# Reordering the first pair of an attention kernel: maxima ahead of differences, ScalarE's order by hand

## The chip, the cores and the metric

The kernel runs on one core of a Trainium2 chip. Its time is that of one execution on the device, in microseconds (us), from runs of the whole program. The core has five engines, each with its own queue of instructions: TensorE (PE in the profile; PEld is its loading of weights), VectorE (DVE), ScalarE (ACT), GpSimd (POOL) and SyncE (SP). SP only issues DMAs; ScalarE and GpSimd can issue them too (ACTq, and POOL's queue).

## The reference

Attention with a mask in blocks of 64, and behind it a gated MLP with a last projection:

```python
scores = scale * np.matmul(q, k.transpose(0, 1, 3, 2))     # q, k, v: 8 batches, 8 heads, 576, 64
scores = np.where(block_i >= block_j, scores, -1e9)        # blocks of 64 positions
scores = scores - np.max(scores, axis=-1, keepdims=True)
attn = np.exp(scores)
attn = attn / (np.sum(attn, axis=-1, keepdims=True) + 1e-09)
x = np.matmul(attn, v)                  # then laid out as 4608 tokens x 512
a = x @ w1                              # 512 x 1024
b = x @ w2                              # 512 x 1024
h = a * b @ w3                          # 1024 x 1024
return h @ w_out                        # 1024 x 512
```

The weights come as 64-bit floats; q, k and v as 32-bit floats.

## The kernel before, in words

**Work and stages.** The heads are taken in 32 pairs, four to a batch. A pair's two heads (j = 0, 1) lie in the two halves of the partitions. The first four pairs (EARLY) run beside the loading and unpacking of the weights; then the weights' working space is closed, and 28 pairs run with the MLP of the batch before filling TensorE. The MLP of the last batch ends the program. w3 and w_out are multiplied with each other once, in the early stage (gen_prod), so that the MLP has three weights: w1, w2 and the product w.

**A pair.** shift_mask(n) casts k (kb) and q (qd) to 16 bits on ScalarE, multiplies them in six groups (tiles mx) and takes each block's maximum on VectorE (line 196); a transpose (mt), a negation on ScalarE (ms, line 202) and shift put the negated maxima into rows of the tile qk. In pair 0, shift is a product on VectorE with rows of constants (line 213); in the others it is a small DMA on ScalarE's queue (line 218). prep_qk(n, j) casts q and k into a high part (line 166, VectorE), copies that to the other half (lines 229 and 230 in pair 0, DMAs at 232 and 233 in others) and forms the low part by a difference (line 235). s_tiles makes the scores in five tiles (line 265, two products for each part) with exponentials on ScalarE (line 273, pe). pv_early multiplies them with the values (line 304; ve holds the values and a half of ones that gives the sums). take_early, norm and finish_x divide and split the result.

**Weights.** load_w takes one load of 512 KB: a DMA on SP into one of five buffers wraw, two passes on ScalarE (lines 150 and 151), one on GpSimd (152) and one on VectorE (153). There are 40: eight of w_out (tile wo), sixteen of w3 (two for each of eight blocks m, in two buffers), and eight each of w1 and w2, whose values are split into a high and a low part on GpSimd and VectorE (161, 162). gen_w hands them out in order: before, w_out first, then w3's first two blocks, then w1, w2 and further blocks of w3 as their buffers come free. gen_prod multiplies block by block; one step is two products (four matmul records in the profile), 32 steps in all.

**Order.** TensorE's order is that of the program's text (manual_schedule). For the other engines a planner orders the instructions by priority and by its own model of time; steps of the early pairs have a raised priority, weights haven't. The order around a pair is written out by hand in a string for each head: B is a step of prep_qk(n, 1), M of shift_mask(n + 1), A of prep_qk(n + 1, 0), S a tile of scores, V a value product, C a step of gen_w, W a step of gen_prod, Q the values' casts of the next pair and the load of the pair after it, N and T the end of a head and of the pair. Ahead of the first pair stands:

```python
    fill(shift_mask(0), 100)
    fill(prep_qk(0, 0), 100)
    for j in range(2):
        prep_v(0, j)
    weights = gen_w(wp)
    fill(weights, 2)
    load(1)
```

fill(g, k) takes k steps of g. A step of gen_w before is two loads.

## Time and profile before

| what | value |
|---|---|
| time, median of 3 runs (lowest to highest) | 971.45 us (969.41 to 972.49) |
| the profiled execution: time, span | 970.15 us, 968.3 us |
| mean granted TensorE clock | 0.996 |
| busy, share of the span: TensorE, VectorE, ScalarE, GpSimd | 97%, 72%, 57%, 64% |
| TensorE busy in the first 20 us | 4.9 us |
| TensorE busy from 20 to 120 us | 88.8 us |
| TensorE busy from 140 to 900 us | all of it |
| first matmul of the MLP (line 426) | at 137.17 us |
| DMA engines busy, first 60 us | 80% to 99% in each 10 us |

The profile comes from one execution, 1.3 us under the median. Its span runs from the first to the last instruction; the time has 1.85 us around it. All times in rows are us from the start of the span. A row of the timeline gives start, duration, engine, line, operation, the tiles out<-in, their shape, how many instructions are merged, and in brackets how long the engine was idle before, with what ended that. A busy TensorE is not TensorE at its peak, since matmuls overlap.

### The profile page before, as it was taken

Reading aid. Unit: us, or ns where it says so; the run is one execution under the profiler, and the core shown is the slowest. Engines: PE = TensorE matmul, PEld = TensorE weight load, DVE = VectorE, ACT = ScalarE, POOL = GpSimd, SP = SyncE. Lnnn points to the kernel's source line nnn. Section 1 sums busy time; section 2 is a strip of 40 time slices with the busy share of each in tenths; the row PEclk is TensorE's granted clock in tenths of the full one; section 3 lists DMA queues with packets and bytes.
Section 4 is the critical chain, followed back from the end, with each engine's and each line's share of the span. In section 5 each row is a group of like instructions: output and inputs, shape, how many; then the busy total and the mean of one; then the engine's idle time right before and its main releaser. Section 6 shows DMA issues by size and latency. Waiting matters only on the chain.

```text
span 968.3 us, 18335 instructions
## 1 busy us (share of the span) xinstructions
PE 938.8 (97%) x6624; PEld 878.7 (91%) x6624; DVE 692.3 (72%) x1230; ACT 556.6 (57%) x1451; POOL 617.5 (64%) x605
## 2 busy tenths in 40 slices
PE   3898899999999999999999999999999999999998
PEld 1454469999999999999999999999999999999998
DVE  6787767788777777787787777777887777774100
ACT  7768736556565556565656555565555656553221
POOL 6766737677766767677776767676777667672211
PEclk9899999999999999999999999999999999999999
DMA  8976512212212221321222222222122122100000
GB/s 303 305 230 204 158 51 64 86 32 72 76 58 82 65 88 52 88 65 47 66 76 64 71 81 64 78 61 88 33 69 75 58 82 64 50 13 26 7 20 26
DMA packets 31303, 79.81 MB, mean 82 GB/s; under 512 B 5356, under 2 KB 13676, under 8 KB 31212
## 3 DMA queue, kind: packets, MB, share of 16 engines
q1 hardware_dynamic: 29788, 76.26, 25.7%
q10 hardware_dynamic: 1424, 2.38, 1.0%
q8 instruction: 52, 0.85, 0.4%
q14 instruction: 39, 0.32, 0.1%
HBM read 50.76 MB, written 9.44 MB: 62 GB/s over the span
## 4 chain that ended last, share of the span: by engine, by line
PE 89%; ACT 3%; DVE 3%; POOL 2%; issue 1%; DMA 1%; ACTq 0%; SPq 0%; DVEq 0%; POOLq 0%
PE ab L426 42%; PE o L442 21%; PE s L265 9%; PE x L320 9%; PE mx L192 4%; PE w L407 2%; POOL wbits L152 1%; ACT wbits L151 1%; ACT wy L150 1%; PE x L304 1%; DVE m L196 1%; ACT pe L273 1%; DMA qk<-ms 1%; DVE w L153 0%; PE tot L337 0%
## 5 line engine op out<-in xcount | busy, mean ns | idle before, releaser
L286 POOL TENSOR_TENSOR rsum<-rsum,p 128x448 f32<-128x448 f32 x224 | 185.8, 829 | 86.8 <-ACT p L280 78.3
L283 DVE TENSOR_TENSOR pl<-p,ph 128x448 fp32r<-128x448 f32 x168 | 149.4, 903 | 59.9 <-ACT ph L281 59.0
L435 POOL TENSOR_TENSOR gl<-g,gh 128x288 fp32r<-128x288 f32 x128 | 114.4, 894 | 121.9 <-ACT gh L434 121.9
L265 PE MATMUL s<-qk 128*128 128x288 f32 (+4 forms) x768 | 155.2, 311 | 6.1 <-ACT pe L273 3.6
L235 POOL TENSOR_TENSOR qk<-raw,qk 64x1152 fp32r<-64x1152 f32 x58 | 155.0, 2673 | 8.6 <-issue 5.6
L426 PE MATMUL ab<-xh,w2h 128*128 128x288 f32 x512 | 153.8, 300 | 0.0
L442 PE MATMUL o<-gh,wh 128*128 128x288 f32 x512 | 153.6, 300 | 0.0
L426 PE MATMUL ab<-xh,w1h 128*128 128x288 f32 x512 | 151.1, 295 | 0.0
L426 PE MATMUL ab<-xl,w2h 128*128 128x288 f32 x512 | 151.0, 295 | 0.0
L426 PE MATMUL ab<-xl,w1h 128*128 128x288 f32 x512 | 151.0, 295 | 0.0
L426 PE MATMUL ab<-xh,w1l 128*128 128x288 f32 x512 | 150.9, 295 | 0.0
L426 PE MATMUL ab<-xh,w2l 128*128 128x288 f32 x512 | 150.9, 295 | 0.0
L442 PE MATMUL o<-gh,wl 128*128 128x288 f32 x512 | 150.9, 295 | 0.0
L442 PE MATMUL o<-gl,wh 128*128 128x288 f32 x512 | 150.8, 295 | 0.0
L434 ACT CAST gh<-g 128x288 fp32r<-128x288 f32 x128 | 55.4, 433 | 143.1 <-DVE g L433 143.0
L265 PEld LDWEIGHTS s<-qk 128*128 128x128 f32 (+1 forms) x768 | 116.0, 182 | 17.9 <-ACT pe L273 9.4
L281 ACT ACTIVATE ph<-s 128x288 fp32r<-128x288 f32 x336 | 131.5, 393 | 0.0
L196 DVE TENSOR_REDUCE m<-mx 128x1 f32<-128x64 f32 (+3 forms) x320 | 128.4, 447 | 2.2 <-PE mx L192 0.2
L280 ACT ACTIVATE p<-s 128x448 f32<-128x448 f32 x224 | 85.4, 381 | 51.2 <-PE s L265 50.4
L283 DVE TENSOR_TENSOR pl<-rsum,ph 128x288 fp32r<-128x288 f32 x112 | 75.6, 676 | 49.6 <-ACT ph L281 45.6
L320 PE MATMUL x<-ph,vs 128*128 128x128 f32 x336 | 110.4, 329 | 0.0
L433 DVE TENSOR_TENSOR g<-ab,a 128x288 f32<-128x288 f32 x128 | 56.6, 442 | 69.8 <-PE ab L426 69.0
(76 smaller groups left out, 2180.4 us busy)
## 6 DMA issues: line engine op xcount, KB each, us to landing
raw<-in_qkv SPq DMA_DIRECT2D x31, 896.0 KB
qk<-qk SPq DMA_DIRECT2D x108, 144.0 KB
out_t<-o SPq DMA_DIRECT2D x64, 144.0 KB
wraw<-in_w3t SPq DMA_DIRECT2D x16, 512.0 KB
wraw<-in_w SPq DMA_DIRECT2D x16, 512.0 KB
wraw<-in_wout SPq DMA_DIRECT2D x8, 512.0 KB
qk<-qk ACTq DMA_DIRECT2D x16, 144.0 KB
qk<-ms SPq DMA_DIRECT2D x54, 2.2 KB
```

The source lines that it names most:

```text
L196: nc.vector.reduce_max(m[:, col : col + 1], sc, axis=AX.X)
L235: (nc.gpsimd if "late" in tl or n * j else nc.vector).tensor_tensor(out=qk[j][o, 2:4], in0=rqk[o], in1=qk[j][o, 0:2], op=ALU.subtract)
L265: nc.tensor.matmul(t[ks, at : at + q1 - q0], qk[j][:, k, kr], qk[j][:, q, q0:q1], start=(s == 0), stop=(s == 1))
L280: nc.scalar.activation(p32, t[ks, at : at + w], AF.Exp, scale=SCALE)
L281: nc.scalar.activation(ph[ks, o : o + w], t[ks, at : at + w], AF.Exp, scale=SCALE)
L283: nc.vector.tensor_tensor(out=low, in0=p32, in1=ph[ks, o : o + w], op=ALU.subtract)
L286: nc.gpsimd.tensor_tensor(out=r, in0=r, in1=p32, op=ALU.add)
L320: nc.tensor.matmul(xps[:, to : to + w], v[:, c, :], pr[:, a : a + w], start=(u < 2 and s == 0), stop=(u in (0, len(PV) - 1) and s == len(p ...
L426: nc.tensor.matmul(t[:, 0:HALF], l[:, c, fs], r, start=(c == 0 and s == 0), stop=(c == NC - 1 and s == 2))
L433: nc.vector.tensor_tensor(out=g32, in0=acc[1][:, 0:HALF], in1=a32, op=ALU.mult)
L435: nc.gpsimd.tensor_tensor(out=gl[:, f, :], in0=g32, in1=gh[:, f, :], op=ALU.subtract)
L442: nc.tensor.matmul(t[:, 0:HALF], l[:, f, es], r[:, f, :], start=(f == 0 and s == 0), stop=(f == NF - 1 and s == 2))
```

## The change

It touches the start and the first two pairs.

- The constants' rows (144 KB for each of two tables) went by SP into a scratch tile and by four copies on GpSimd into the tiles qk; now two DMAs on GpSimd's queue write them straight into qk, one for each head and both tables (288 KB each).
- The differences of pair 0 move from VectorE to GpSimd (both heads), and the copies of head 0 from ScalarE to VectorE.
- The values of pairs 0 and 1 are loaded apart from q and k, later (load_v).
- From the casts of pair 0 to the end of its first head ScalarE too is kept in the order of the text. The first six groups of maxima stand in it, then head 0's prep_qk, then two weight loads (the first block of w3), then the rest of the shift.
- In pair 0's first head three score tiles stand ahead of the masks of pair 1, and these are cut finer (a step before each cast of q).
- gen_w steps by one load (c; C is two), hands out w3's first two blocks first, then w_out, and further blocks of w3 as soon as their buffer allows. Ahead of pair 0 there are two loads instead of four; pair 0 takes eight in both, so ten instead of twelve have been handed out by its end.
- gen_prod takes blocks 0 and 1 together, row by row of w_out, so that its first step needs both blocks of w3 and one row of w_out. Pair 0 has four W instead of two, pair 1 eight instead of nine.

```diff
@@ -49,10 +49,10 @@
 )
 
 EARLY_PLAN = (
-    ("B B M S S B M S M S C M S M V V C V V V Q N",
-     "M S S A C S M S A C S V V A M V V V Q N T W W"),
-    ("B B C M S S W B M S S M W C S M W V V M V V V Q N",
-     "M S S A C W S M S A W C S W V V A M V V V C Q N T W W W"),
+    ("B B S S S M V S M V S M B c V M c V M V C M Q N",
+     "S S A C S W M S A S W A M V V W C M V W V M V Q N T"),
+    ("B B C M S S W B M S S M W C S M W V V M W V V V Q N",
+     "M S S A C S M S A C S W V V A M V V W V C Q N T W W"),
     ("B B M S S W C B M S S M W C S M W V V M V V V Q N",
      "M S S A W C S M S A W C S W V V A M V V V Q N T W W W C"),
     ("B B C M S S W B M S S M W C S M W V V M V V V Q N",
@@ -101,17 +101,17 @@
     def load(n):
         t = raws.tile([P, RAW], F32, tag="raw", name=f"raw{n}")
         src = qkv[n // NPAIR, n % NPAIR]
-        for cs in (slice(S, 2 * S), slice(0, S), slice(2 * S, RAW)) if n == 0 else (slice(0, RAW),):
+        raw_of[n] = t
+        for cs in (slice(S, 2 * S), slice(0, S)) if n == 0 else (slice(0, 2 * S),) if n == 1 else (slice(0, RAW),):
             nc.sync.dma_start(out=t[:, cs], in_=src[:, cs])
-        raw_of[n] = t
+
+    def load_v(n):
+        nc.sync.dma_start(out=raw_of[n][:, 2 * S :], in_=qkv[n // NPAIR, n % NPAIR][:, 2 * S :])
 
     load(0)
-    for t, tag in enumerate(("tr", "x32")):
-        cst = work.tile([P, S], F32, tag=tag, name=f"cst{t}")
-        nc.sync.dma_start(out=cst[0:D], in_=consts[:, t * S : (t + 1) * S])
-        for j in range(2):
-            nc.gpsimd.tensor_copy(qk[j][oth[j], 3 * t, :], cst[0:D])
     nc.sync.dma_start(out=both, in_=ident_in)
+    for j in range(2):
+        nc.gpsimd.dma_start(out=qk[j][oth[j], 0:4:3, :], in_=consts.rearrange("p (t s) -> p t s", t=2))
     nc.gpsimd.memset(qd, 0.0)
 
     tl = {}
@@ -177,6 +177,8 @@
         kb = work.tile([P, S], BF16, tag="kb", name=f"kb{n}")
         cast(n, kb, rqk[:, 1, :], CAST[1])
         for j in range(2):
+            if n == 1:
+                yield
             cast(n, qd[own[j], :, own[j]], rqk[own[j], 0, :].rearrange("p (i r) -> p i r", r=BLK), CAST[2])
         yield
         m = work.tile([P, 32], F32, tag="m", name=f"m{n}")
@@ -225,14 +227,14 @@
         cast(n, qk[j][o, 0:2], rqk[o], CAST[0])
         yield
         if n == 0:
-            copy = nc.gpsimd.tensor_copy if j else nc.scalar.copy
+            copy = (nc.gpsimd if j else nc.vector).tensor_copy
             copy(qk[j][x, 1, :], rqk[o, 1, :])
             copy(qk[j][x, 2, :], rqk[o, 0, :])
         else:
             queue(n).dma_start(out=qk[j][x, 1, :].bitcast(F32), in_=qk[j][o, 1, :].bitcast(F32))
             queue(n).dma_start(out=qk[j][x, 2, :].bitcast(F32), in_=qk[j][o, 0, :].bitcast(F32))
         yield
-        (nc.gpsimd if "late" in tl or n * j else nc.vector).tensor_tensor(out=qk[j][o, 2:4], in0=rqk[o], in1=qk[j][o, 0:2], op=ALU.subtract)
+        (nc.gpsimd if "late" in tl or n == 0 or j else nc.vector).tensor_tensor(out=qk[j][o, 2:4], in0=rqk[o], in1=qk[j][o, 0:2], op=ALU.subtract)
         yield
 
     def prep_v(n, j):
@@ -375,42 +377,61 @@
         def rows(u):
             for k in range(2 * u, 2 * u + 2):
                 load_w(tl["wo"][:, k, :], wout[k])
+                yield
 
         def w3(m):
             assert done[0] >= m - 1
             t3_of[m] = wp.tile([P, NF, P], F32, tag="w3", name="w3", bufs=2)
             for h in range(2):
                 load_w(t3_of[m][:, 4 * h : 4 * h + 4, :].rearrange("p k f -> p (k f)"), w3t[2 * m + h])
+                yield
 
         def split(dst_h, dst_l, src):
             g = load_rows(dst_h, dst_l, src)
             return lambda _: next(g)
 
         one, two = split(w1h, w1l, w1), split(w2h, w2l, w2)
+        for m in range(2):
+            yield from w3(m)
         for u in range(4):
-            rows(u)
-            yield
-        m, rest = 0, [one] * 4 + [two] * 4
+            yield from rows(u)
+        m, rest = 2, [one] * 4 + [two] * 4
         while m < NF or rest:
-            if m < NF and done[0] >= m - 1 and (m < 2 or len(rest) <= 9 - m or not rest):
-                w3(m)
+            if m < NF and (done[0] >= m - 1 or not rest):
+                yield from w3(m)
                 m += 1
             else:
                 rest.pop(0)(None)
-            yield
+                yield
+                yield
 
     def gen_prod():
         wo = tl["wo"]
-        for m in range(NF):
-            acc = ps_m.tile([P, 512], F32, tag="psm", name=f"w{m}")
-            for k in range(NF):
-                nc.tensor.matmul(acc, t3_of[m][:, k, :], wo[:, k, :], start=(k == 0), stop=(k == NF - 1))
-                if k % 2 and k < NF - 1:
-                    yield
+
+        def part(acc, m, k):
+            nc.tensor.matmul(acc, t3_of[m][:, k, :], wo[:, k, :], start=(k == 0), stop=(k == NF - 1))
+
+        def out(acc, m):
             nc.scalar.copy(wh[:, m, :], acc)
             nc.vector.tensor_tensor(out=wl[:, m, :], in0=acc, in1=wh[:, m, :], op=ALU.subtract)
             done[0] += 1
+
+        acc = [ps_m.tile([P, 512], F32, tag="psm", name=f"w{m}") for m in range(2)]
+        for k in range(NF):
+            for m in range(2):
+                part(acc[m], m, k)
+            if k == NF - 1:
+                for m in range(2):
+                    out(acc[m], m)
             yield
+        for m in range(2, NF):
+            acc = ps_m.tile([P, 512], F32, tag="psm", name=f"w{m}")
+            for k in range(NF):
+                part(acc, m, k)
+                if k == NF - 1:
+                    out(acc, m)
+                if k % 2:
+                    yield
 
     def gen_moe(b):
         mp, gh, gl = tl["late"], tl["gh"], tl["gl"]
@@ -456,12 +477,17 @@
     wstack = ExitStack()
     wp = wstack.enter_context(tc.tile_pool(name="wp", bufs=1))
     open_early(wp)
-    fill(shift_mask(0), 100)
+    weights = gen_w(wp)
+    first = shift_mask(0)
+    start = tc.manual_schedule(engines={mybir.EngineType.Activation})
+    start.__enter__()
+    fill(first, 7)
     fill(prep_qk(0, 0), 100)
+    fill(weights, 2)
+    fill(first, 100)
+    load_v(0)
     for j in range(2):
         prep_v(0, j)
-    weights = gen_w(wp)
-    fill(weights, 2)
     load(1)
     prod = gen_prod()
 
@@ -481,9 +507,11 @@
             tiles = s_tiles(n, j, p_early)
             pvs = (pv_early if early else pv)(n, j, xps, p_early)
             delay = DELAY if n == NPAIR and j == 0 else 0
+            if n == 0 and j == 1:
+                start.__exit__(None, None, None)
             for step in (EARLY_PLAN[n] if early else PLAN)[j].split():
-                if step in "CW":
-                    fill(weights if step == "C" else prod, 1)
+                if step in "CcW":
+                    fill(prod if step == "W" else weights, 2 if step == "C" else 1)
                     continue
                 with tc.high_priority(offset=0) if early else nullcontext():
                     if step == "S":
@@ -513,6 +541,8 @@
                         norm(n, x32, rr)
                         finish_x(n, x32)
                     elif step == "Q" and not last:
+                        if n == j == 0:
+                            load_v(1)
                         if n + 1 != NPAIR:
                             prep_v(n + 1, j)
                         if j == 1 and n + 2 < NN:
```

## The prediction

> **What bounds the kernel now.** I read the page first: the span, and the rows of the 40 slices (24.2 us each).
>
> ```profile
> span 968.3 us, 18335 instructions
> PE   3898899999999999999999999999999999999998
> DMA  8976512212212221321222222222122122100000
> ```
>
> From the sixth slice on TensorE's digit is 9 throughout, so nothing that the change does there can be seen; its early work (attention of four pairs beside the loading of the weights) ends later or sooner, and the part behind is shifted with it. The question is how much idle TensorE loses or wins before that. So I read next TensorE's timeline of the early stage (start, duration, what, and in brackets the idle time before it with what ended it); these are rows picked out of it.
>
> ```profile
> 5.93 1.01 PE L192 MATMUL mx<-kb,qd 128*128 128x512 bf16 x2 [5.93 <-ACT qd L166]
> 15.47 1.09 PE L265 MATMUL s<-qk 128*128 128x288 f32 x3 [0.97 <-DVE qk L213]
> 20.80 0.61 PE L192 MATMUL mx<-kb,qd 128*128 128x512 bf16 x1 [4.24 <-ACT qd L166]
> 28.15 0.80 PE L265 MATMUL s<-qk 128*128 128x288 f32 x4
> ...
> 31.77 0.64 PE L265 MATMUL s<-qk 128*128 128x192 f32 x4 [1.40 <-ACT pe L273]
> 35.64 0.27 PE L200 MATMUL mt<-ident,m 128*9 128x128 f32 x1
> 35.75 1.39 PE L304 MATMUL x<-pe,ve 128*128 128x320 f32 x6
> 37.07 3.70 PE L407 MATMUL w<-wo,w 128*128 128x512 f32 x8
> 41.35 0.64 PE L265 MATMUL s<-qk 128*128 128x288 f32 x3 [0.45 <-DMA qk<-ms]
> 45.78 0.61 PE L192 MATMUL mx<-kb,qd 128*128 128x512 bf16 x1 [2.07 <-ACT qd L166]
> 58.84 0.68 PE L265 MATMUL s<-qk 128*128 128x448 f32 x2 [0.44 <-ACT pe L273]
> 65.33 0.27 PE L200 MATMUL mt<-ident,m 128*9 128x128 f32 x1
> 95.26 0.27 PE L200 MATMUL mt<-ident,m 128*9 128x128 f32 x1
> 103.28 0.66 PE L265 MATMUL s<-qk 128*128 128x288 f32 x3 [1.05 <-DMA qk<-ms]
> ```
>
> The reader is to see three kinds of wait: the first maxima (to 15.47 almost nothing but waiting), the masks of pair 1 standing ahead of the first head's third score tile (4.24 at 20.80), and exponentials or shifts that come late (1.40, 0.45, 2.07). The chain that ended last says which work set the pace. Its lines carry start and duration.
>
> ```profile
> 4.45 1.23 DVE qk L166
> 6.50 1.36 DVE qk L235
> 7.88 1.71 DVE qk L235
> 46.66 1.28 POOL wbits L152
> 61.30 1.03 POOL w1h L161
> 126.31 10.50 PE w L407 x24
> ```
>
> It starts with VectorE's casts and differences, and from 46 us it runs for a while through the unpacking of the weights on GpSimd, which is what speaks against a large gain.
>
> **The change part by part.** 1. *Maxima ahead of differences.* VectorE's, ScalarE's and GpSimd's rows of the start:
>
> ```profile
> 9.62 4.02 DVE L196 TENSOR_REDUCE m<-mx 128x1 f32<-128x512 f32 x10
> 14.67 1.53 DVE L213 TENSOR_TENSOR qk<-ms,qk 9x576 fp32r<-9x576 f32 x2 [0.84 <-ACT ms L202]
> 8.75 0.67 ACT L150 ACTIVATE wy<-wraw 128x512 f32<-128x512 f32 x1 [0.86 <-DMA wraw<-in_wout]
> 10.28 0.67 ACT L150 ACTIVATE wy<-wraw 128x512 f32<-128x512 f32 x1 [0.20 <-DMA wraw<-in_wout]
> 10.85 0.76 ACT L151 ACTIVATE wbits<-wraw 128x512 fp8e4<-128x512 uint8 x1
> 14.30 0.27 ACT L202 ACTIVATE ms<-mt 9x128 fp32r<-9x128 f32 x1 [2.09 <-PE mt L200]
> 35.56 2.87 POOL L235 TENSOR_TENSOR qk<-raw,qk 64x1152 fp32r<-64x1152 f32 x1
> 6.52 5.04 POOL L113 CAST qk<-cst 64x576 fp32r<-64x576 f32 x4 [1.45 <-DMA cst<-in_consts]
> ```
>
> The differences of both heads (1.36 and 1.71) and the second head's cast leave VectorE's way; two copies of 64x576 come to it from ScalarE, each half of a 64x1152 cast of 1.23, so 0.6. VectorE is then free at 4.45 + 1.23 + 1.2 = 6.9, and the maxima's products are there at 5.93 plus half of 1.01. The ten reductions start at 6.9 instead of 9.62: -2.7. Behind them nothing is shortened (9.62 to 15.47 is 5.85), so the first full score product comes at 12.75. Head 0's difference on GpSimd costs 2.87 from 5.7, to 8.6, hidden until 12.75; head 1's (2.87 again), its two copies (5.04 for four of that size, so 2.5) and the first two unpackings (1.28 each) end by about 17, before that head begins at 22. The four copies of the constants (5.04) go, and two DMAs on GpSimd's queue come, at 288 KB each; before, both tables together were 288 KB on SP. Nothing in this trace shows the landing of a DMA from that queue: they must land before the shift's rows are made, at 14.67 - 2.7 = 12.0; I take nothing, as tables that queued on SP were there by 6.52, with +2 as the far end (the wait that 6.52 shows for the constants, 1.45, rounded up) and no gain, since nothing else waits for them. By hand, ScalarE's negation of the maxima stands behind the first two weight loads. These began at 8.75 and 10.28 and ended at 11.61 (10.85 + 0.76), and the negation is due at 14.30 - 2.7 = 11.6: nothing. The bytes ahead of the loads are about the same (288 + 288 + 128 KB on SP and 576 on GpSimd, 1280, against 1312), because the values of pair 0 now come behind these two loads; each us that the second load is late costs one. The values are needed only by the first value product, behind three score tiles.
>
> 2. *Scores and values of the first head ahead of the masks.* The 4.24 of waiting goes. What is late next is the same cast, now between the exponentials on ScalarE: the first mask group stands behind the third value product and waits for the exponential of the last tile and one cast of 0.67. I take 0.9 for all waits of this head (ends 0 and 4.24; nearest is the cast's own length): -3.35. The second head's scores come at 28.15 - 2.7 - 3.35 = 22.1.
>
> 3. *ScalarE's order.* These are its rows at the change of heads, and the cost of a load on it (least, median, most in ns):
>
> ```profile
> 28.79 0.71 ACT L273 ACTIVATE pe<-s 128x288 f32<-128x288 f32 x2
> 29.39 0.63 ACT L346 COPY x<-x 64x576 f32<-64x576 f32 x1
> L150 ACT ACTIVATE wy<-wraw x21: 646/665/681, 8.7 to 60.0; 128x512 f32<-128x512 f32 x21
> L151 ACT ACTIVATE wbits<-wraw x20: 762/774/791, 9.3 to 57.8; 128x512 fp8e4<-128x512 uint8 x20
> ```
>
> A load is 0.67 + 0.77, some 1.25 with the overlap of neighbours (10.28 to 11.61 is 1.33). In the first head four loads come behind the last exponential, 5.0, and the values' cast and the output copy (0.63) behind them, about 6 in all. ScalarE's last mask cast ends some 1.8 before that head does (three mask groups and two short value products stand behind it; an estimate), at 20.3. If the second head's exponentials stand behind all of the 6, ScalarE is free at 26.3 and the first one done at 26.7, while TensorE has done two tiles (0.80) at 22.9 and waits for a buffer: 3.7. If they go between the loads, TensorE waits for the first weight rows at its first product step: two loads of w3 and one of wout, 3 x 1.25, and two exponentials of 0.36 from 20.3, which is 24.8, then about 1 for GpSimd's and VectorE's part, 25.75, against 23.9 behind the third tile: 1.85. I take +1.85 (ends 0 and 3.7), because in the rows above exponentials do go ahead of loads. The product steps between the scores fill the wait of 1.40 in that head: -1.4.
>
> 4. *The cover at the end of pair 0.* Before, two product steps (3.70) and the last values (1.39) lie between the transpose at 35.64 and pair 1's scores, while the shift's DMA travels. After, all four product steps come ahead of the transpose. The rows of that DMA's issue:
>
> ```profile
> 37.34 1.31 ACTq L218 DMA_DIRECT2D qk<-ms  x1
> 97.34 0.78 ACTq L218 DMA_DIRECT2D qk<-ms  x1
> ```
>
> From issue to the product that needs it: 41.35 - 37.34 = 4.0 and 103.28 - 97.34 = 5.9; lower end 2.9 (the DMA can have been there at 40.2). With 0.35 for the negation and without 0.5 of cover left, 4.0 gives 3.85 of wait, and 0.45 was there: +3.4 (ends +2.3 and +5.3). I take 4.0, the same pair's. Two steps of work are done earlier for it; they are not lost, but they pay nothing here.
>
> 5. *Pair 1.* In that wait ScalarE has time for pair 2's mask casts: the 2.07 at 45.78 goes (ends 0 and -2.07). The second head's scores lose the product steps between them: its wait of 0.44 becomes more like the 1.40 of the head that had none: +1.0 (ends 0 and +1.4).
>
> 6. *The rest.* The product has 32 steps in both; two blocks begun together need the same matmuls, and 24 matmul records at the end (10.50) become 20. Pairs 2 and 3 keep nine and eight steps and ten and eight loads; the last two loads come behind pair 3, while the product's end (still 8.7) covers them. Without it they would cost two loads of 1.25 and their GpSimd parts of 1.28 and 1.03, some 4. Nothing.
>
> Sum: -2.7 - 3.35 + 1.85 - 1.4 + 3.4 - 2.07 + 1.0 = -3.3. The profiled execution took 970.15 (span 968.3), so 966.9; the median of the three runs is 971.45 and their spread 3.1, so against the median it is -4.5, 0.47%. A difference under 0.3% (2.9 us) can't be told from none in this kernel.
>
> *The clock.* The granted clock halves twice in the early stage (columns: TensorE, its loads, VectorE, ScalarE, GpSimd busy, then the clock):
>
> ```profile
> 32.00:34.00 2.00, 2.00 (x8) 1.47 (x8) 2.00 (x3) 2.00 (x6) 0.90 (x1) 0.52 0.98 365
> 46.00:48.00 2.00, 2.00 (x7) 1.53 (x7) 1.40 (x3) 1.94 (x4) 1.86 (x2) 0.50 0.56 219
> ```
>
> Each stands behind a wait, that of 1.40 and that of 2.07. I leave two such stretches in the sum, behind the new waits of 1.85 and 3.85. The Trainium skill ("TensorE: Matmul & The Clock Gate", Part 1) says that the clock halves after an idle window of about 3.4 us and comes back after as long a busy one. The trace does not agree on the first: waits of 1.4 and 2.1 were enough. By that rule only the wait of 3.85 could bring a stretch, one where there were two; one stretch, 1.7 as priced with the rivals, would be won, and the time 965.2.
>
> **The rivals.** *ScalarE's hand order blocks the second head.* All that is ahead in program order runs first: 3.7 instead of 1.85, and behind a wait that long one more half-clock stretch, 1.7 (an estimate: each row above holds nearly two us at half speed, worth one, and the stretches reach beyond the rows): 966.9 + 3.55 = 970.5, no change. For it speaks that the order is fixed by the program's text; against it that it ends with the first head.
>
> *The weights' stream sets the pace.* It is the case on the other side. By the end of pair 0 ten loads have been issued instead of twelve. The chain runs through unpacking at 46.66 and 61.30. A pair takes 29.9 (transposes at 65.33 and 95.26) and ten loads, 3.0 a load: two loads late are +6.0, so 972.9, slower than before. Three late, since the split loads of w1 and w2 now crowd into the later pairs, are 975.9. It undoes the gain from 1.1 loads (3.3 / 3.0), and shows as slower from 2.5. Against it: the DMA row falls from 9 to 5 over the first slices, so later loads can catch up, and w3 is loaded more eagerly.
>
> *The shift's transfer is as slow as pair 3's.* 5.9 for 4.0, and the halved clock behind it a little longer (up to 1.7): 966.9 + 1.9 + 1.7 = 970.5, no change. It speaks for it that the DMA engines are busiest in these slices; against it that pair 1's own was 4.0.
>
> *By the clock rule above*, 965.2.
>
> **How the numbers follow.** Forecast 966.9 (own range 963.5 to 968.5): 0.40. The clock case, 0.08. ScalarE's order, 0.18. The slow shift, 0.12. The stream, 0.22: 0.08 with two loads or fewer, within what can't be told from no change, and 0.14 with more. Faster 0.40 + 0.08 = 0.48; no change 0.18 + 0.12 + 0.08 = 0.38; slower 0.14. The range, 963.5 to 973.5, reaches from the gains' good ends (0 for the wait of 1.85 and a little of the shift's) to the stream's case of two loads, and leaves out its worse part and a bit below, 2 in 10.
>
> **What would show it.** Right: reductions starting near 6.9, the first full score product near 12.75, no wait over 1 us for pair 1's mask casts, a wait of 3 to 4 for the shift at pair 1's first scores, and TensorE's first MLP product (137.2 before, where the full part starts) near 134. Wrong: ScalarE running loads while the second head's scores wait, product steps waiting for weights after 46 us, or the constants' DMA landing behind 12.0.

## The result: slower by 0.9%, and the profile after

The changed kernel took 980.62 us (median of 6 runs, 976.6 to 982.3) against 971.09 for the kernel before on the same chip (6 runs, 968.45 to 972.93): ratio 1.0094, interval 1.0068 to 1.0121. Forecast were 966.9 and a range up to 973.5. The profiled execution took 980.11 us against 970.15. One of the six executions of a_shift (below) took 1948.88 us, twice as long as any other, and is left out there, which makes its median 979.54 (979.68 with it). The page's rows of the changed kernel:

```profile
span 978.2 us, 18333 instructions
PE   4679899999999999999999999999999999999998
DMA  8857722222222122122222221221222222100000
```

The digits for TensorE are higher in the first slice (4 for 3) and lower in the second and third (6 and 7 for 8 and 9): the start is fuller and then something is empty. From the sixth slice both kernels are the same. TensorE's timeline of the early stage, rows picked out:

```profile
17.46 2.22 PE L267 MATMUL s<-qk 128*128 128x288 f32 x5 [3.22 <-DVE qk L215]
24.56 0.39 PE L194 MATMUL mx<-kb,qd 128*128 128x512 bf16 x1 [0.60 <-ACT qd L166]
26.57 0.85 PE L267 MATMUL s<-qk 128*128 128x288 f32 x4
30.64 1.11 PE L267 MATMUL s<-qk 128*128 128x448 f32 x2 [3.22 <-ACT pe L275]
44.43 0.27 PE L202 MATMUL mt<-ident,m 128*9 128x128 f32 x1
53.62 1.06 PE L267 MATMUL s<-qk 128*128 128x288 f32 x3 [8.22 <-POOL xl L370]
74.38 0.27 PE L202 MATMUL mt<-ident,m 128*9 128x128 f32 x1
102.45 0.27 PE L202 MATMUL mt<-ident,m 128*9 128x128 f32 x1
112.80 0.66 PE L267 MATMUL s<-qk 128*128 128x288 f32 x3 [3.38 <-DMA qk<-ms]
136.28 0.28 PE L202 MATMUL mt<-ident,m 128*9 128x128 f32 x1
```

The MLP's first matmul is at 146.93, 9.76 later than before, and that is nearly all of the difference of the spans (9.9). The same stage as groups, with the waits of each group behind the last bar; first the kernel before, up to its first MLP product, then the changed one:

```profile
L265 PE MATMUL s<-qk 128*128 128x288 f32 (+4 forms) x99 | 26.4, 384 | 6.1 <-ACT pe L273 3.6 <-DMA qk<-ms 1.5 <-DVE qk L213 1.0
L192 PE MATMUL mx<-kb,qd 128*128 128x512 bf16 (+7 forms) x50 | 13.5, 343 | 19.2 <-ACT qd L166 12.2 <-DVE m L196 6.9
...
L267 PE MATMUL s<-qk 128*128 128x288 f32 (+4 forms) x100 | 26.6, 382 | 22.2 <-POOL xl L370 8.2 <-ACT pe L275 7.3 <-DMA qk<-ms 3.4
L194 PE MATMUL mx<-kb,qd 128*128 128x512 bf16 (+7 forms) x50 | 12.4, 320 | 12.3 <-ACT qd L166 6.8 <-DVE m L198 5.4
```

The waits of the mask products shrank by 6.9 us, as meant. The waits of the score products grew by 16.1. The net, 9.2, is nearly all of the 9.76.

To see where, the transposes (mt, one at the end of each pair) must be compared net of the product steps that lie ahead of them, 1.85 us each. Before, 0, 8, 17 and 26 steps are done at the four transposes; after, 4, 9, 18 and 27.

| stretch | later than before | steps ahead, us | net |
|---|---|---|---|
| first full score product | +1.99 | 0 | +2.0 |
| second head's scores | -1.58 | 0 | -1.6 |
| transpose in pair 0 | +8.79 | 7.4 | +1.4 |
| pair 1's first scores with shift | +12.27 | 3.7 | +8.6 |
| transpose in pair 1 | +9.05 | 1.85 | +7.2 |
| in pair 2 | +7.19 | 1.85 | +5.3 |
| in pair 3 | +11.47 | 1.85 | +9.6 |

So the start lost 2.0, the first head won 3.6, the second lost 3.0, the shift behind pair 0 lost 7.2, pairs 1 and 2 won back 3.3, and pair 3 lost 4.3. Some work only changed places in these rows. Two of the three value products that stood behind pair 0's transpose stand ahead of it now (0.86 us), so of the second head's 3.0 some 0.9 belongs to the shift, which then lost 8.1; and two small mask groups moved from the first head to the second.

**The start.** VectorE's and GpSimd's rows, VectorE first:

```profile
5.00 0.75 DVE L166 CAST qk<-raw 64x1152 fp32r<-64x1152 f32 x1
6.25 3.07 DVE L166 CAST qk<-raw 64x1152 fp32r<-64x1152 f32 x1
9.36 4.01 DVE L198 TENSOR_REDUCE m<-mx 128x1 f32<-128x512 f32 x10
14.34 4.20 DVE L215 TENSOR_TENSOR qk<-ms,qk 9x576 fp32r<-9x576 f32 x2 [0.78 <-ACT ms L204]
5.84 2.86 POOL L237 TENSOR_TENSOR qk<-raw,qk 64x1152 fp32r<-64x1152 f32 x1 [1.19 <-DVE qk L166]
14.18 2.61 POOL L237 TENSOR_TENSOR qk<-raw,qk 64x1152 fp32r<-64x1152 f32 x1
```

Two things are to be seen. The planner put the second head's cast (6.25) ahead of the reductions, which so begin at 9.36 and not at 6.9. And that cast takes 3.07 where the same cast took 0.75 at 5.00: it ends 0.62 after GpSimd's difference (5.84 + 2.86 = 8.70, and 6.25 + 3.07 = 9.32). The first shift product at 14.34 likewise ends at 17.41, 0.62 after the second difference (14.18 + 2.61 = 16.79). Both look as if VectorE had stood still while GpSimd's difference ran, and the scores waited for it (a_diff below tests this).

**The second head, and the shift.** ScalarE's rows, in order; DMA issues on its queue are ACTq:

```profile
24.53 0.69 ACT L150 ACTIVATE wy<-wraw 128x512 f32<-128x512 f32 x1
...
28.65 0.78 ACT L151 ACTIVATE wbits<-wraw 128x512 fp8e4<-128x512 uint8 x1
29.27 0.45 ACT L246 COPY ve<-raw 128x320 f32<-128x320 f32 x1
29.61 0.69 ACT L150 ACTIVATE wy<-wraw 128x512 f32<-128x512 f32 x1
30.18 0.41 ACT L275 ACTIVATE pe<-s 128x288 f32<-128x288 f32 x1
...
45.02 0.67 ACT L150 ACTIVATE wy<-wraw 128x512 f32<-128x512 f32 x1
45.59 0.44 ACT L246 COPY ve<-raw 128x320 f32<-128x320 f32 x1
46.06 0.27 ACT L204 ACTIVATE ms<-mt 9x128 fp32r<-9x128 f32 x1
46.40 1.31 ACTq L220 DMA_DIRECT2D qk<-ms  x1
47.75 0.63 ACT L348 COPY x<-x 64x576 f32<-64x576 f32 x1 [0.62 <-DVE rb L359]
47.84 0.74 ACTq L220 DMA_DIRECT2D qk<-ms  x1
```

From 24.53 to 30.18 ScalarE runs four loads, the values' cast and a fifth load's first pass; only then comes the second head's first exponential, while TensorE waits 3.22. At the end of pair 0 the transpose is done at 44.70, but the negation runs at 46.06, behind a weight pass and a cast; and the first of the two shifts on the queue is that of pair 1's second head. The first head's, which TensorE needs, goes out at 47.84 and is used at 53.62, 5.8 later. The wait's row names xl, which is only the latest semaphore seen; in a_act, a_diff and a_load below the same wait is put down to the shift's DMA. The rows do not tell the two shifts apart; the order comes from the instructions of the program as built.

### The profile page after: what moved, and what is told of

It is laid out like the page before. It is cut to its first block, busy times and chain, and to the rows that moved or that the text cites. A ratio compares the mean times of both kernels' runs of the same rounds, so it can differ in the third digit from the quotient of the medians.

```text
span 978.2 us, 18333 instructions
## 1 busy us (share of the span) xinstructions
PE 939.4 (96%) x6624; PEld 879.0 (90%) x6624; DVE 701.7 (72%) x1230; ACT 555.7 (57%) x1449; POOL 621.9 (64%) x605
## 4 chain that ended last, share of the span: by engine, by line
PE 86%; DVE 1%; ACT 0%; issue 0%; POOL 0%; DVEq 0%; ACTq 0%
PE ab L447 42%; PE o L463 21%; PE s L267 9%; PE x L322 9%; PE mx L194 4%; PE w L412 1%; PE tot L339 0%; PE mt L202 0%; PE x L306 0%; DVE m L198 0%; DVE w L153 0%; DVE tr L346 0%; ACT wbits L151 0%; DVE qk L166 0%; POOL w2h L161 0%
## 5 line engine op out<-in xcount | busy, mean ns | idle before, releaser
L237 POOL TENSOR_TENSOR qk<-raw,qk 64x1152 fp32r<-64x1152 f32 x60 | 160.6, 2677 | 3.7 <-DVE qk L166 1.2
```

The costliest lines, as they stand in the source:

```text
L237: (nc.gpsimd if "late" in tl or n == 0 or j else nc.vector).tensor_tensor(out=qk[j][o, 2:4], in0=rqk[o], in1=qk[j][o, 0:2], op=ALU.subtract)
```

## Experiments

Kernels whose name begins with a start from the changed kernel, with b from the kernel before. Each ratio is to the kernel before on the same chip, whose median was 970.88 us beside the first four, 971.61 beside the next four, 970.78 beside the four from b_warm to a_shift, and 971.13 beside the last two. The ratios are estimated from all the runs and differ by up to 0.12% from those of the medians. The intervals of a_cover, a_act, a_diff, a_load and a_shift overlap that of the changed kernel (1.0068 to 1.0121), so small differences from it are not shown by the times alone.

| kernel | edit | us | ratio, interval |
|---|---|---|---|
| a_cover | two product steps back behind pair 0's transpose | 977.73 | 1.0061, 1.0039 to 1.0083 |
| a_act | no order by hand on ScalarE | 977.24 | 1.0056, 1.0037 to 1.0074 |
| a_diff | differences back on VectorE | 982.25 | 1.0114, 1.0086 to 1.0142 |
| b_nocover | before, without its cover | 978.01 | 1.0064, 1.0038 to 1.0090 |
| a_load | one more C (two loads) in pair 1 | 980.72 | 1.0095, 1.0068 to 1.0121 |
| a_cover_act | a_cover and a_act | 972.50 | 1.0012, 1.0000 to 1.0023 |
| b_first | before, first head's scores first | 975.37 | 1.0035, 1.0023 to 1.0048 |
| b_prod | before, two blocks at once | 974.64 | 1.0028, 1.0015 to 1.0041 |
| b_warm | before, unread products in waits | 971.82 | 1.0006, 0.9994 to 1.0018 |
| b_first_warm | b_first, the same | 975.03 | 1.0032, 1.0017 to 1.0047 |
| c_warm | a_cover_act, the same | 972.45 | 1.0014, 1.0003 to 1.0026 |
| a_shift | second head's shift on GpSimd's queue | 979.54 | 1.0081, 1.0066 to 1.0095 |
| d_noprod | a_cover_act with the old product | 974.51 | 1.0026, 1.0009 to 1.0043 |
| a_cover_act_diff | all three | 971.60 | 1.0004, 0.9994 to 1.0014 |

**a_cover.**

```diff
-     "S S A C S W M S A S W A M V V W C M V W V M V Q N T"),
+     "S S A C S W M S A S W A M V V C M V M V V Q N T W W"),
```

> The changed kernel with one line of the plan undone in part: in pair 0's second head two of the four product steps go back behind the last value product, between the transpose and pair 1's scores. Theory 'cover' (most of the loss is the 8.2 us for which pair 1's second score product waits for the shift's DMA): that wait falls from 8.2 to under 2.5, and the time from 980 to 973 to 975, less the two steps' work that now lies there. Rival 'stream' (the weights set the pace anyway): the wait falls, but TensorE's first MLP product stays within 2 us of 146.9 and the time near 979. Rival 'start' (ScalarE's hand order and GpSimd beside VectorE cost it): 978 or more, since neither is touched.

977.73, 2.9 below the changed kernel. The wait for the shift is gone, but a wait of 2.42 for the last maxima came at the transpose, where the steps had stood. The two steps there took 6.09 where 3.70 had been the price before. So this cover was worth less than the wait that it filled: what it left behind opened another, and the steps themselves ran slower.

**a_act.**

```diff
-    start = tc.manual_schedule(engines={mybir.EngineType.Activation})
+    start = nullcontext()
```

> The changed kernel without ScalarE's hand order (the planner orders it throughout); all else as changed. Theory 'start': the wait of 3.2 us for the second head's first exponential (30.6 us) goes or halves, and with it the stretch of halved clock behind it; 3 to 6 us less, 974 to 977. Theory 'cover': the uncovered shift still costs some 8 us, so the time stays above 976 whatever the second head gains.

977.24, 3.4 below. The wait for the second head's exponentials fell from 3.22 to 0.56; the wait for the shift stayed, and here its row names the DMA. A new wait of 2.19 for the last maxima came at the transpose of pair 0.

```profile
48.59 1.06 PE L267 MATMUL s<-qk 128*128 128x288 f32 x3 [8.22 <-DMA qk<-ms]
```

**a_diff.**

```diff
-        (nc.gpsimd if "late" in tl or n == 0 or j else nc.vector).tensor_tensor(...)
+        (nc.gpsimd if "late" in tl or n * j else nc.vector).tensor_tensor(...)
```

> The changed kernel with pair 0's differences back on VectorE. Theory 'port' (GpSimd's difference and VectorE's cast and shift products hold each other up: 3.07 us for a cast of 0.75, 4.20 for two products of 0.75): the cast takes 0.75 and the two products 1.5 again, the reductions begin near 9.7 as before, and the first full score product comes at 15.5 to 16 instead of 17.5; the time falls by about 2, to 978. If contention is not the cause, the long instructions stay long and the score product comes later than 17.5, since VectorE has 3 us more to do.

The second head's cast and the first shift product are short again:

```profile
7.91 0.76 DVE L166 CAST qk<-raw 64x1152 fp32r<-64x1152 f32 x1
15.37 0.75 DVE L215 TENSOR_TENSOR qk<-ms,qk 9x576 fp32r<-9x576 f32 x1 [0.77 <-ACT ms L204]
```

So GpSimd's difference was what had held them up. The first full score product came at 16.18, 1.28 sooner, yet the time did not fall (it is 1.6 higher, with intervals that overlap): the second head waited 4.35 for exponentials, the shift 8.62. The gain ahead of a wait that ScalarE sets only made the wait longer here.

**b_nocover.**

```diff
-     "M S S A C S M S A C S V V A M V V V Q N T W W"),
-    ("B B C M S S W B M S S M W C S M W V V M V V V Q N",
+     "M S S A C S M S A C S V V A M V V V Q N T"),
+    ("B B C M S S W W W B M S S M W C S M W V V M V V V Q N",
```

> The kernel before with one thing of the change alone: the two product steps behind pair 0's last value product are moved behind pair 1's first two score tiles, so that nothing lies between the transpose and these scores; number and order of all other steps as before. Theory 'cover': pair 1's second score product now waits 4 to 8 us for the shift's DMA where it waited 0.45; the two steps (3.7 us) still come, so 3 to 6 us of it are lost and the time is 974 to 977. Rival 'stream': the weights are late anyway, the wait shows up but waits after it shrink, 971 to 972.

Moving two product steps by two score tiles costs the kernel before 7.1 us. Its first scores of pair 1 then wait 4.31 for the shift at 45.32. That is near the prediction's 3.85 by luck: from the end of the transpose (36.56) to that product 8.8 us pass, where the prediction had 4.35, and 4.4 of them lie under the first score product and the last values, which wait 0.61 and 1.48 for exponentials. The three product steps behind it take 7.10, with a clock of 0.50 and 0.56 from 46 to 50 us, and the start was 0.65 later in this execution. So here the missing cover cost more than the wait that it uncovered.

**a_load.**

```diff
-    ("B B C M S S W B M S S M W C S M W V V M W V V V Q N",
+    ("B B C M S S W C B M S S M W C S M W V V M W V V V Q N",
```

> The changed kernel with one more C in pair 1's first head, so that two more loads of weights have been handed out from there on, twenty-two by the end of pair 1 as before the change, and none is left over behind pair 3. Theory 'late loads' (pair 3 takes 33.8 us from transpose to transpose where it took 29.6, because the stream is two loads behind): pair 3 shrinks by 2 to 4 us and the time falls to 976 to 978; the wait at pair 1 stays at 8. Rival 'order' (the order of w1, w2 and w3 loads, not their number, makes pair 3 long): pair 3 stays near 33.8 and the time within 1.5 us of 980.

The time did not move (980.72 against 980.62). The wait at pair 1 was 7.39, and pair 3 still took 33.3, though its shift waited only 1.55 there. The rival of the weights' stream, priced by the loads handed out late, falls.

**a_cover_act.** Both edits above.

> The changed kernel with two product steps back behind pair 0's last values, and without ScalarE's hand order. Alone the first gave 977.7 and the second 977.2. If these are two separate losses, both come back: the wait for the shift under 1 us, the second head's exponential wait under 1 us, 973.5 to 975.5, with pair 3's 4 us left against before. If the one only moves to where the other was (rival 'one bottleneck'), 976 to 977.5.

972.50, 8.1 below the changed kernel, where the two alone give 2.9 and 3.4, and below the 973.5 that the expectation had as its best: each loss had been covered in part by the other. The kernel is back at the kernel before, and no better; VectorE's last maxima of pair 0 now make TensorE wait 5.17 at the transpose:

```profile
39.29 0.38 PE L202 MATMUL mt<-ident,m 128*9 128x128 f32 x1 [5.17 <-DVE m L200]
37.08 2.15 DVE L200 TENSOR_TENSOR m<-m 128x1 f32<-128x1 f32 x1
36.61 2.60 POOL L237 TENSOR_TENSOR qk<-raw,qk 64x1152 fp32r<-64x1152 f32 x1 [0.76 <-DVE qk L166]
```

The second row is the last step of those maxima, 2.15 us for 128 numbers (0.16 at 13.40 in the changed kernel). It is GpSimd's difference again: it ends at 36.61 + 2.60 = 39.21, and the step at 39.23. Some 2 of the 5.17 are that.

**b_first and b_prod.** Parts of the change alone, in the kernel before. In b_first only pair 0's first plan is changed; in b_prod gen_w and gen_prod are those of the changed kernel, C stands for two of the finer steps and four stand ahead of pair 0.

```diff
-    ("B B M S S B M S M S C M S M V V C V V V Q N",
+    ("B B S S S M V S B V S M V M C V M C V M Q N",
```

> The kernel before with one thing of the change alone: in pair 0's first head three score tiles and the first value products stand ahead of pair 1's masks (one string of the plan). The prediction's second step says that 3.35 us of TensorE's wait for the mask casts go and stay won: 967 to 968.5, a wait at 20.8 of under 1 us. Rival 'given back': the head is shorter but a later wait takes it (the exponentials of the second head, or the shift's transfer, behind the same weight loads), 970 to 972.

> The kernel before with the weights' part of the change alone: w3's first two blocks ahead of w_out, further blocks of w3 as soon as allowed, and the product begun with two blocks at once; start, plan and number of loads as before. Theory 'late loads': with the number of loads kept, pair 3 stays near 29.6 and the time within 2 us of 971. Rival 'order': w1 and w2 crowd into the later pairs, pair 3 takes 32 to 34 and the time is 974 to 976.

Both are slower, by 3.8 and by 3.0. For b_first theory and rival were both too low. There 1.02 is left of the 4.24 of waiting, and a wait of 3.11 for the second head's last exponentials comes at 41.92; the transposes are 1.9, 3.1, 3.8 and 5.5 us later than before. Pairs 2 and 3, whose plans are the same, take 0.7 and 1.7 longer; why is not shown. b_prod has the time of its rival, but its pair 3 takes 31.2, not 32 to 34: pair 0 is 1.2 shorter, and pairs 1, 2 and 3 are each some 1.7 longer. In pair 2 the product waits for VectorE to empty its accumulator:

```profile
70.20 7.11 PE L410 MATMUL w<-wo,w 128*128 128x512 f32 x12 [2.86 <-DVE wl L414]
```

**Unread products in the waits.** A natural suspect was the clock, which the prediction's two rows have at 0.52 and 0.50 behind waits. Three kernels keep TensorE busier.

```diff
+    still = cpool.tile([P, P], BF16, name="still")
+    nc.vector.memset(still, 0.0)
...
+        for _ in range(k):
+            nc.tensor.matmul(t, still, still.unsqueeze(1).broadcast_to([P, 4, P]), start=True, stop=True)
```

> The kernel before with products put into TensorE's waits that nothing reads (bf16, 128 x 512, on a tile of zeros): 10 ahead of pair 0's first mask product, 8 behind the second, 2 ahead of the transpose, 8 in the wait of 4.24 us at 20.80, 4 in that of 1.40 at 31.77, 8 in that of 2.07 at 45.78. Theory (a good part of what waits cost is the half clock that follows them): the two half stretches at 32.4 and 46.0 (3.4 us each, nearly all of it busy) and the slow products up to 24.7 (a pair of 512-column mask products takes 1.01 there, one takes 0.38 later) go: 1.5 + 1.5 and up to 1 at the start, 967 to 969. Rival (the waits are set by ScalarE, VectorE and loads, faster products only wait longer, and the planner's own order shifts by the added instructions): 970 to 973.

> The kernel before with the scores and values of the first head ahead of the masks (as in the run that had 975.37), and unread products in TensorE's waits of pair 0 as above. There TensorE waited 27.0 us in all ahead of the first MLP product, only 0.7 more than in the kernel before, but its half stretches were 20.4 us against 6.8. Theory (the gain of step 2 was given back in the half clock): the stretches at 27.8 (10.2) and 41.4 (6.8) go, 967 to 970. Rival (the second head waits on ScalarE and VectorE anyway: waits of 3.11 for the exponentials and 1.4 for the maxima, which faster products only lengthen): 973 to 976.

> The changed kernel with cover at the end of pair 0 and without ScalarE's order by hand (972.5), and unread products in the waits of pair 0: at the start, ahead of the first scores (2.67), and 16 ahead of the last transpose of pair 0 (wait of 5.17 at 39.29). Theory (half clock): the stretch at 36.0 (6.8, of which 3.5 busy) goes, -1.7, and the products up to 22 run at full clock, -1: 969.5 to 970.5; the stretches of pairs 2 and 3 stay. Rival (VectorE's maxima end at 39.2 whatever the clock, and head 0's shift lands at 47.0 behind them): 972 to 973. A candidate to beat the kernel before.

None moved: 971.82, 975.03 and 972.45 against 970.78, 975.37 and 972.50. In b_warm and c_warm half stretches stay, at other places, so they decide little. In b_first_warm they did go where b_first had its longest one. The windows from 20 to 45 us (length, then TensorE, its loads, VectorE, ScalarE and GpSimd busy, the mean clock, the share and rate of the DMAs), b_first above:

```profile
20.00:45.00 25.00, 16.66 (x53) 10.05 (x52) 17.96 (x31) 18.84 (x38) 17.32 (x15) 0.72 0.90 280
20.00:45.00 25.00, 20.47 (x83) 11.22 (x82) 17.57 (x29) 17.36 (x36) 16.49 (x15) 0.93 0.93 296
```

The clock rises from 0.72 to 0.93 and the time stays. Faster products there only wait longer for ScalarE and VectorE (the first mask product within pair 1, at 48.97, waits 2.87 for a cast). The half clock is not what took b_first's gain; the rival of that expectation holds.

**a_shift.**

```diff
-        queue(n).dma_start(out=row.bitcast(F32), in_=ms_of[n]...)
+        (nc.gpsimd if n == j == 1 else queue(n)).dma_start(out=row.bitcast(F32), in_=ms_of[n]...)
```

> The changed kernel with the shift of pair 1's second head issued on GpSimd's queue, so that ScalarE issues the first head's shift without the other one ahead. Theory (the wait of 8.22 is 3.85 predicted + 1.36 for a late negation + 1.44 for the wrong shift first + 1.6 of travel): the wait falls to 6.5 to 7, 978.5 to 979.5. Rival (what sets it is the travel behind the loads of pair 3's inputs and weights, or VectorE and GpSimd now busier): wait still above 8, 980 to 981.

> The changed kernel with the shift of pair 1's second head on GpSimd's queue, for its profile alone (979.68 when timed, 0.9 below the changed kernel). Theory (order on ScalarE's queue costs 1.44 of the wait of 8.22): the wait for the shift is 6.5 to 7.3 and the first head's shift is issued within 0.6 of the negation's end. Rival: the wait stays above 8 and the 0.9 comes from elsewhere.

979.54, 1.1 below the changed kernel, though the two intervals overlap. The timeline is that of a_shift2, the same kernel run once more for its profile (976.06 in that one execution). ScalarE's, TensorE's and VectorE's rows:

```profile
43.23 1.32 ACTq L220 DMA_DIRECT2D qk<-ms  x1
48.62 1.06 PE L267 MATMUL s<-qk 128*128 128x288 f32 x3 [6.47 <-DMA qk<-ms]
15.18 2.22 PE L267 MATMUL s<-qk 128*128 128x288 f32 x5 [0.90 <-DVE qk L215]
L215 DVE TENSOR_TENSOR qk<-ms,qk x2: 751/1912/3072, 14.4 to 15.2; 9x576 fp32r<-9x576 f32 x2
```

The wait fell by 1.75 to 6.47 once the other shift was off the queue; 5.4 of travel stay. The last two rows show something not asked for. Here the first shift product took 0.75 and the second 3.07, and the first scores came at 15.18, 2.3 sooner than in the changed kernel, by chance: VectorE began at 14.37 and GpSimd's difference at 14.38,

```profile
14.37 3.85 DVE L215 TENSOR_TENSOR qk<-ms,qk 9x576 fp32r<-9x576 f32 x2 [0.77 <-ACT ms L204]
14.38 3.24 POOL L237 TENSOR_TENSOR qk<-raw,qk 64x1152 fp32r<-64x1152 f32 x1
```

while in the changed kernel GpSimd had begun 0.16 ahead of VectorE. In these two traces the one that starts first keeps the other out for its whole length. This execution is 2.28 ahead of the changed kernel's at the first scores, 3.25 at pair 0's transpose, 5.00 at pair 1's scores and 4.33 at the MLP's first matmul. It is a single one, and part of the 4.05 by which it is below 980.11 is that chance at the start.

**d_noprod and a_cover_act_diff.**

> The changed kernel's start, casts, masks and first head's order, with the weights' product, its loads and the plans' product steps as in the kernel before (none ahead of pair 0's last transpose, two behind it) and without ScalarE's order by hand. Against the run with cover and without the order by hand (972.5) only the product's early steps are out, which alone cost the kernel before 3.0 (974.64 against 971.61). Theory A (that cost is what keeps 972.5 from being a gain): 969 to 970.5, faster than the kernel before. Theory B (the first head's order is what costs, 3.8 alone in the run that had 975.37, and early product steps fill its waits): 973.5 to 976.

> The kernel with cover and without ScalarE's order by hand (972.5), with pair 0's differences back on VectorE ahead of the reductions. Alone that brought the first full score product from 17.46 to 16.18 and in the end 1.6 us of loss. Theory (start gains reach the end once the two waits behind are gone): 971 to 971.8. Rival (the last maxima of pair 0 on VectorE at 39.2 and the shift behind them set the pace, a start gain is given back there): 972 to 973.5.

d_noprod took 974.51, theory B: with the old product it is about as slow as b_first. So the product's early steps, a loss alone, seem to be none beside the new order of the first head, whose waits they fill: d_noprod is 2.0 above a_cover_act, with intervals that overlap.

a_cover_act_diff took 971.60, 0.9 below a_cover_act, with intervals that overlap too. It does not test its theory, because it had no start gain to carry on: the first full score product came at 17.23, as in a_cover_act (17.24).

```profile
17.23 2.22 PE L267 MATMUL s<-qk 128*128 128x288 f32 x5 [2.15 <-DVE qk L215]
```

VectorE was not held up by GpSimd, but without the order by hand ScalarE ran pair 1's mask casts ahead of the negation, which began at 16.13 (14.04 in the changed kernel). What differs is the transpose of pair 0, which waits 2.79 instead of 5.17. The kernel is within 0.1% of the kernel before.

No version beat that kernel, and pair 3 stands in the way of those that have both the cover and the new product. Net of the one more product step, the transpose in pair 2 comes 1.7 us sooner than in the kernel before in a_cover_act (95.40 for 95.26 + 1.85) and 3.0 sooner in a_cover_act_diff (94.16); then pair 3 takes 33.8 in both where it took 29.6, and the lead is gone.

## Why the prediction was wrong, step by step

Four terms of the sum failed: step 1 was +2.0 for -2.7, step 4 +7.2 for +3.4, step 3 +3.0 for +0.45, and step 6, put at nothing, +2.4. Steps 2 and 5 held. Of the signs that the prediction named for being wrong, the first came: ScalarE ran loads from 24.53 to 30.18 while the second head's scores waited.

1. *Maxima ahead of differences*, forecast -2.7 (first full score product at 12.75), was +2.0 (17.46). The step failed in two assumptions: that the second head's cast leaves VectorE's way (the planner put it ahead of the reductions, at 6.25), and that GpSimd's differences are hidden beside VectorE's work (they stopped VectorE twice, for 2.3 each time, 3.07 less 0.75). The reductions began 2.46 later than forecast and the second stop came on top; that is the miss of 4.7. a_diff shows the stops by taking them away. The trace before had the sign: its first cast, 1.23 at 4.45, ended 0.62 behind GpSimd's copy (4.40 + 0.66 = 5.06), while the next one, 0.77 at 5.71, had no GpSimd instruction beside it, and the prediction took 1.23 as the plain price. The Trainium skill ("SBUF — State Buffer", section "Who interferes with whom") says that a VectorE cast in a two-port mode, or a VectorE instruction with two inputs in SBUF, contends with a GpSimd instruction that reads SBUF, and that whoever issues first has the shared ports for the whole instruction. The traces agree, with 3.07 for 0.75 and with the two orders of start at 14.2 to 14.4. The constants' DMAs, a worry of that step, were not late: they landed by 10.6 at the latest, where 12.0 was the limit.
2. *The first head's scores ahead of the masks*, forecast -3.35, was -3.57 (from 17.46 to 26.57, 9.11 against 12.68; a little of it is the two mask groups that moved): right, and the wait for the mask cast was 0.60. But right in its place only: b_first shows that alone it makes the kernel slower by 3.8.
3. *ScalarE's order*, forecast +1.85 and -1.4, was +3.0 (2.1 without the value products that moved). It is the first rival, nearly to the number: a wait of 3.22 (3.7 was its price). Taking +1.85 because exponentials go ahead of loads in the trace before was the error; that order came from the planner, and here the text ruled.
4. *The cover at the end of pair 0*, forecast a wait of 3.85 (ends 2.75 and 5.75), was 8.22. The mechanism was right and the size off. The prediction's sum was 0.35 from the transpose to the issue, 4.0 of travel, less 0.5 of cover. Measured were 3.14 (44.70 to 47.84), 5.78 and 0.70, which make the 8.22. Of the 3.14, 1.36 is the wait of the negation behind ScalarE's weight pass and cast, and 1.44 the other head's shift ahead on the queue (a_shift2 won 1.75 without it); neither was in the range. The travel of 5.8 is that of the third rival, which had 5.9. Two readings of the prediction's own rows were wrong as well: in the kernel before, 1.43 pass from the end of the transpose (35.64 + 0.27) to the issue at 37.34, not 0.35; and the DMA can't have been there at 40.2, since the wait of 0.45 at 41.35 ended with it. Which shift goes first is the planner's choice, and it changes with the cover: in the programs as built the second head's is first in the changed kernel, a_act, a_diff, a_load and b_nocover, which have no product steps behind pair 0's transpose, and the first head's in the kernel before and in all others that have them. Why it does so is not shown.
5. *Pair 1*, forecast -1.07, was -1.4: no wait over 1 us for pair 2's mask casts, right.
6. *The rest*, forecast 0, was -1.9 in pair 2 and +4.3 in pair 3. Two loads handed out late are not it (a_load). In pair 3 of the changed kernel the shift waits 3.38 (1.05 before) for this chain on ScalarE:

```profile
105.39 0.68 ACT L150 ACTIVATE wy<-wraw 128x512 f32<-128x512 f32 x1 [1.78 <-DVE w1l L162]
106.10 0.27 ACT L204 ACTIVATE ms<-mt 9x128 fp32r<-9x128 f32 x1
106.39 0.78 ACTq L220 DMA_DIRECT2D qk<-ms  x1
```

The transpose was done at 102.72, but the negation stood behind a load that waited for VectorE. The wait grew by 2.3, but it does not make the pair long: it is 1.92 in a_act and 1.55 in a_load, and pair 3 takes 33.8 and 33.3 there. Pair 3 took 33.3 to 33.8 in every timeline with the changed plans and the new product together, 29.6 in the kernel before, 31.2 with the product alone (b_prod), 31.5 with the old product and the new start (d_noprod), and 31.1 and 31.3 in b_nocover and b_first. What grows with it is the unpacking of weights on GpSimd, here within pair 3, before the change and after it:

```profile
L152 POOL TENSOR_SCALAR wbits<-wraw 128x512 uint8<-128x512 uint8 x8 | 9.1, 1131 | 1.2 <-DMA qk<-ms 0.6
L152 POOL TENSOR_SCALAR wbits<-wraw 128x512 uint8<-128x512 uint8 x12 | 14.3, 1193 | 5.4 <-issue 4.1 <-DVE w L153 0.6
```

GpSimd is busy for 18.1 us of pair 3 before and 24.7 after; in a_load for 22.5, with ten unpackings. So work on the weights has moved from pairs 1 and 2 into pair 3, which is the half of the stream rival that says that the loads of w1 and w2 crowd into the later pairs. That this sets the length of the pair is not shown, since no run changed it alone: the cause of pair 3's 4.3 stays open.

Sum up to the MLP: forecast -3.3, measured +9.6. Of the miss of 12.9, 7.0 lies ahead of pair 0's transpose (4.7 at the start, 2.5 in the second head, -0.2 in the first), 3.8 at the shift, 2.1 behind it; with the value products that moved, the second head has 1.6 and the shift 4.7. The second rival, the weights' stream, gave a time of that sign; its price for each late load fell with a_load, and its crowding of the later pairs is open. The forecast of two half-clock stretches held in number; their cost is not the cause, as far as b_first_warm can tell.

## What to carry to other kernels

Before moving an instruction to another engine, look in the trace for what runs on VectorE at that moment and whether GpSimd reads on-chip memory beside it: here 0.75 us became 3.07, and a start 0.16 us sooner decided who waited. Price each "hidden" transfer by the whole queue in front of it (the instructions ahead of its source, the other transfers ahead of it, then its travel), since a cover that is taken away uncovers all three. And when three engines are each some 70% busy (72%, 75% and 69% in b_first's window above), a wait removed on one of them comes back on the next: test a part alone before adding its gain to a sum.

## What was not expected of the hardware

- A VectorE cast of 64x1152 and a product of 9x576 took 3.07 beside GpSimd's difference and 0.75 alone, a step on 128 numbers 2.15 and 0.16: each ended as if it had begun only 0.13 to 0.15 ahead of GpSimd's end.
- Shifts of 2.2 KB took from 4.0 us (pair 1 of the kernel before) to 6.4 (pair 3 of the changed one) from issue to use.
- With a mean clock of 0.93 in place of 0.72 over 25 us, the time did not move.
